# Chunk attention and a two-layer network in one kernel: other block sizes, other early order, transposing DMA from unit 7 on

## The chip, the cores and the metric

The kernel runs on one core of a Trainium2 chip. Its time is the device time of one execution in microseconds; the median of the runs is given. The profile is a separate execution, recorded by the hardware profiler.

## What is computed

Attention inside chunks of 64 positions, for 8 batches, 8 heads, 576 positions and 64 values a head; the heads are then laid side by side to 512 features for 4608 tokens, which go through two matrices with a leaky ReLU between them.

```python
scores = scale * np.matmul(q_c, k_c.transpose(0, 1, 2, 4, 3))   # chunks of 64
scores = scores - np.max(scores, axis=-1, keepdims=True)
attn = np.exp(scores)
attn = attn / (np.sum(attn, axis=-1, keepdims=True) + 1e-09)
out = np.matmul(attn, v_c)
...
x = np.ascontiguousarray(attn_out.transpose(0, 2, 1, 3)).reshape(B * S, H * D)
h = x @ w_in                      # 512 to 2048
g = np.maximum(0.01 * h, h)
return (g @ w_out)                # 2048 to 512
```

## The kernel before

The tokens are cut into 36 units of 128 (two chunks). Each unit goes through stages that the program names with letters:

- **tq, tk**: TensorE transposes q and k into the PSUM tiles qp and kp (one buffer each). **q** copies qp in two halves into QZ, a zero-padded operand, and **k** copies kp into KT, on ScalarE (ACT) or VectorE (DVE). From unit 9 (`UD`) on, q and k come another way: a DMA lays them out and DVE's own transposes (**dq**, **dk**) write QZ and KT.
- **s**: eight matmuls of 64 columns give the scores Sp. **m**, **b**: DVE takes the maximum and subtracts it. **x**: ACT takes the exponential. **z**: DVE sums, adds 1e-9 and inverts (three instructions). **n**: DVE multiplies, which gives the weights en.
- The weights are transposed in one of two ways. Units below `UE`: **e** (four TensorE transposes into tpe) and **c** (a copy out of PSUM into et, ACT or DVE). Units from `UE` on: **d**, one transposing DMA from SP's queue, en to et.
- **v**: eight matmuls of 64 columns of et with V give xp, which shares its one PSUM buffer with tpe. **a**: ACT copies xp into xT, and from then on the unit's tokens count as ready.

The network works on blocks of 128, 256 or 512 tokens (`BLOCKS`). A block is cut into chunks, also called quarters here: `mm1` (4 x 512 columns of the first layer, 16, 8 or 4 matmuls by the size of the block; its activation `act1` on ACT follows) and `mm2` (four matmuls of 512 columns, a quarter of a token tile's second layer). After the fourth quarter `store` copies the tile out of PSUM on ACT and SP's queue stores it. The last tile of all is done by `last`, in pieces. A chunk is 2048 columns whatever the block. There are 288 of them in a list, and a chunk can be taken when all tokens of its block are ready. hT, oP and the idle matmuls share four PSUM buffers.

The order on each engine is the order of the program. It has three stretches. `FRONT` is an order written out by hand: the stages of the first units, `y` and `w` (zeroing), `I` (the identity in fp32, for unit 0), `A`, `G`, `B`, `O` for single chunks of the first blocks (mm1, act1, mm2, store), and `i12`, which is twelve matmuls on the identity whose results are not used. `q1.0.1` means unit 1, half 0, on ACT. Then rounds `it` from 6 to 38 follow: in a round come s, m, b of unit it-1, `fill(2)`, the exponential, the transposes of the next unit's q and k, z and n, another `fill(2)` and `fill(QUARTERS[it] - 4)`, so that `QUARTERS[it]` chunks are taken in a round if the tokens are there. The values (v and a) of a unit come one round after n for units below `UE`, and in the middle of the round after that for the others:

```python
if it - 3 >= UE:
    values(it - 3)
...
if it - 2 < UE:
    values(it - 2)
```

After the rounds `fill(len(chunks))` takes what is left.

The loads are issued on GpSimd's queue in the order of `LOADS`, before all; only unit 0's q and k (q_f, k_f, fp32) come by SP's and ACT's queues.

Of the kernel before, what the change touches and what calls it, by code (L numbers as in the profile page):

```python
# [11 lines left out]
AFT = mybir.ActivationFunctionType  # L12
# [4 lines left out]
def kernel(  # L17
# [9 lines left out]
    nc = tc.nc  # L27

    B, H, S, D = q.shape
    d_model, d_ff = moe_w_in.shape  # L30
# [8 lines left out]
    NVB = 2  # L39
    NIN = 9  # L40
    UD = 9
    UE = 9
    G = 2 * CH

    NU = n_tok // G
    BLOCKS = [128] * 6 + [256] + [128] * 2 + [256] * 5 + [512] * 4

    sbp = ctx.enter_context(tc.tile_pool(name="k_sb", bufs=1))
    psp = ctx.enter_context(tc.tile_pool(name="k_ps", bufs=1, space=bass.MemoryType.PSUM))
# [6 lines left out]
    w_outT = sbp.tile([128, NFC, d_model], FP16, name="w_outT")  # L56
# [87 lines left out]
    oP: dict[tuple[int, int], bass.AP] = {}  # L144
    START = [sum(BLOCKS[:j]) for j in range(len(BLOCKS))]

# [3 lines left out]
    def mm1(j, a):  # L150
        tb, r0 = BLOCKS[j], START[j]
        nf = 512 // tb
        hT = psp.tile([128, nf, tb], FP32, name="hT", tag="mm", bufs=4)
        for i in range(nf):
            fc = nf * a + i
            for t in range(NT):
                nc.tensor.matmul(  # L157
                    out=hT[:, i, :],
                    lhsT=w_inT[:, t, fc * 128:(fc + 1) * 128],
                    rhs=xT[:, t, r0:r0 + tb],  # L160
                    start=(t == 0),
                    stop=(t == NT - 1),
                )
        HT[j, a] = hT

    def act1(j, a):
        tb = BLOCKS[j]
        nf = 512 // tb
        if j not in gT:
            tag, bufs, pad = ("gS", 4, 128) if tb == 128 else ("gT", 2, 512)  # L170
            gT[j] = sbp.tile([128, NFC, tb], FP16, name="gT", tag=tag, bufs=bufs, padded_shape=[128, NFC, pad])
        nc.scalar.activation(  # L172
            out=gT[j][:, nf * a:nf * a + nf, :], in_=HT.pop((j, a)), func=AFT.Prelu, bias=0.0, scale=1.0, alpha=0.01
        )
# [20 lines left out]
        nc.sync.dma_start(out=out[r0:r0 + 128, :], in_=osb)  # L195

    def last(j, ti):
        r0, c = START[j] + ti * 128, d_model // 2
        osb = sbp.tile([128, d_model], FP32, name="osb", tag="osb", bufs=3)
        for h in range(2):  # L200
            o = psp.tile([128, d_model], FP32, name="oP", tag="mm", bufs=4)
            for fc in range(NFC):
                nc.tensor.matmul(  # L203
                    out=o[:, :c],
                    lhsT=gT[j][:, fc, ti * 128:(ti + 1) * 128],
                    rhs=w_outT[:, fc, h * c:(h + 1) * c],
                    start=(fc == 0),
                    stop=(fc == NFC - 1),
                )
            half = slice(h * c, (h + 1) * c)  # L210
            nc.scalar.activation(out=osb[:, half], in_=o[:, :c], func=AFT.Copy, bias=0.0, scale=1.0)  # L211
            nc.sync.dma_start(out=out[r0:r0 + 128, half], in_=osb[:, half])

    def c1(j):
        return [("mm1", j, a, 0) for a in range(NFC * BLOCKS[j] // 512)]

    def c2(j):
        return [("mm2", j, ti, p) for ti in range(BLOCKS[j] // 128) for p in range(NFC // 4)]

    chunks = []  # L220
    for j in range(len(BLOCKS)):
        chunks += c1(j) + c2(j)
    state = {"tokens": 0}

    def fill(n):
        for _ in range(n):
            if not chunks:
                return
            kind, j, a, p = chunks[0]
            if START[j] + BLOCKS[j] > state["tokens"]:  # L230
                return
            chunks.pop(0)
            if kind == "mm1":
                mm1(j, a)
                act1(j, a)
            elif j == len(BLOCKS) - 1 and a == BLOCKS[j] // 128 - 1:
                if p == 0:
                    last(j, a)
            else:
                mm2(j, a, p)  # L240
                if parts[j, a] == NFC // 4:
                    store(j, a)
# [176 lines left out]
    def zero_act(i):  # L419
# [8 lines left out]
            )  # L428

    FRONT = (  # L430
        "y0 y1 y2 y4 w3 I y5 i12 tq0 tk0 q0.1.1 q0.0 tq1 k0.1 q1.0.1 i4 s0 tk1 m0 k1 b0 q1.1.1 i23 s1 x0 "
        "m1 b1 z0 x1 z1 i55 tq2 q2.0.1 n0 i7 tk2 k2 q2.1 i3 e0 n1 c0.1 s2 m2 i3 v0 a0 b2 i12 e1 x2 c1 i9 "
        "v1 z2 A0.0 a1 A1.0 n2 G0.0 e2 A0.1 c2 v2 tq3 a2 A1.1 q3.1 G0.1 q3.0 tk3 A2.0 G1.0 k3.1 G1.1 s3 "
        "A0.2 G2.0 m3 A1.2 b3 x3 A2.1 G0.2 z3 A0.3 G1.2 tq4 G2.1 n3 A1.3 G0.3 e3 G1.3 A2.2 c3 q4.0.1 v3 "
        "tk4 a3 A2.3 k4.1 q4.1 A3.1 y6 G2.3 G2.2 A3.0 G3.1 s4 A3.3 m4 A3.2 b4 G3.3 G3.0 B0.1 G3.2 B3.1 x4 "
        "B0.0 z4 B1.1 n4 B3.0 B1.2 B0.3 tk5 tq5 k5.1 B0.2 q5.1.1 e4 B1.0 O0 c4 q5.0 B1.3 O1 "
    )
    STAGES = {
        "tq": stage_tq, "tk": stage_tk, "q": stage_q, "k": stage_k, "s": stage_s, "m": stage_m, "b": stage_b,
# [6 lines left out]
    def do(name, u):  # L446
        if (name, u) not in done:
            STAGES[name](u)
# [18 lines left out]
    def values(u):  # L467
        if 0 <= u < NU:
            do("v", u)
            do("a", u)  # L470

    QUARTERS = [5] * 8 + [6] * 9 + [7] * 30
    for it in range(6, NU + 3):
        dve = UD <= it < NU
        if it <= NU:
# [5 lines left out]
        fill(2)  # L481
        if it - 3 >= UE:
            values(it - 3)
        if it <= NU:
            do("x", it - 1)
        if it - 2 < UE:
            do("e", it - 2)
# [9 lines left out]
        if it <= NU:  # L497
            do("z", it - 1)
            do("n", it - 1)
            if it - 1 >= UE:  # L500
                do("d", it - 1)
        fill(2)
        if it - 2 < UE:
            values(it - 2)
        fill(QUARTERS[it] - 4)
        for b in range(3, B):
# [33 lines left out]
```

## Time and profile before

| what | value |
|---|---|
| median of 3 runs | 294.11 us (294.11 to 294.14) |
| profiled execution | 294.1 us, its span 292.3 us |
| matmuls, weight loads | 2556 each |
| TensorE busy | 284.4 us |
| VectorE, ScalarE, GpSimd busy | 182.7, 152.5, 119.4 us |
| first matmul, last matmul group | 3.80 us, 285.41 to 288.92 us |

The span runs from the first to the last instruction; 1.8 us of the execution lie around it. A row of the timeline or of the chain begins with its start and its length in microseconds. Matmuls are pipelined, so the length of a single one is longer than its step in a series; the steps are read from the chain, where the ends of a series are set against each other.

### The profile page before, as it was taken

What the parts mean: (1) busy time and instruction counts of PE and PEld (TensorE: products, weight loads), DVE (VectorE), ACT (ScalarE), POOL (GpSimd) and SP (SyncE); (2) the same over time, 40 slices, a digit from 0 to 9 for tenths busy, and PEclk for the clock granted to TensorE, in tenths of its full rate; (3) what the DMA queues carried; (4) which work ended last, traced back from release to release, by engine and by line L of the source; (5) the groups of instructions that cost most, each with busy time, mean ns of one, the idle gap of its engine ahead of it and who ended that gap; (6) DMA issues with size and microseconds to landing.
All of it is one profiled execution on the core that took longest, in us unless ns stands there. A gap on an engine that the chain in (4) does not pass through costs nothing.

```text
span 292.3 us, 6210 instructions
## 1 busy us (share of the span) xinstructions
PE 284.4 (97%) x2556; PEld 181.8 (62%) x2556; DVE 182.7 (63%) x338; ACT 152.5 (52%) x270; POOL 119.4 (41%) x148
## 2 busy tenths in 40 slices
PE   4999999999999999999999999999999999999995
PEld 3989955878677766767676754444454444444444
DVE  5776536879899898888877888787777720000000
ACT  5457713756456545646454547733763387127511
POOL 8857547898509837920394379210000000000000
PEclk9999999999999999999999999999999999999999
DMA  9999999999999999999499999992111320120022
GB/s 131 162 193 194 202 157 184 168 144 146 127 126 61 148 147 135 139 132 99 66 135 138 105 85 148 94 137 90 56 23 31 112 69 0 38 88 21 0 74 72
DMA packets 192332, 32.00 MB, mean 109 GB/s; under 512 B 183472, under 2 KB 187824, under 8 KB 192304
## 3 DMA queue, kind: packets, MB, share of 16 engines
q0 software_dynamic: 170208, 18.10, 114.0%
q1 hardware_dynamic: 21056, 13.24, 19.4%
q8 instruction: 20, 0.33, 0.4%
q10 hardware_dynamic: 1040, 0.26, 0.4%
q14 instruction: 8, 0.07, 0.1%
HBM read 36.70 MB, written 9.44 MB: 158 GB/s over the span
## 4 chain that ended last, share of the span: by engine, by line
PE 97%; POOL 1%; ACT 1%; issue 1%; DVE 0%; POOLq 0%
PE hT L157 43%; PE oP L182 41%; PE Sp L309 3%; PE xp L376 3%; PE idle L396 3%; PE oP L203 1%; PE qp L259 1%; PE tpe L351 1%; PE kp L259 1%; POOL k_in L69 0%; DVE QZ L274 0%; ACT KT L281 0%; ACT QZ L272 0%; POOL q_in L69 0%; ACT osb L211 0%
## 5 line engine op out<-in xcount | busy, mean ns | idle before, releaser
L157 PE MATMUL hT<-xT,w_inT 128*128 128x128 f16 (+2 forms) x1152 | 134.3, 273 | 0.0
L182 PE MATMUL oP<-w_outT,gT 128*128 128x512 f16 x560 | 128.2, 379 | 0.0
L157 PEld LDWEIGHTS <-w_inT 128*128 128x128 f16 x1152 | 90.0, 98 | 32.7
L172 ACT ACTIVATE gT<-hT 128x512 f16<-128x512 f32 x144 | 83.8, 597 | 32.5 <-PE hT L157 32.3
L182 PEld LDWEIGHTS <-gT 128*128 128x128 f16 x560 | 52.3, 98 | 56.3
L193 ACT ACTIVATE osb<-oP 128x512 f32<-128x512 f32 x35 | 20.9, 596 | 64.6 <-PE oP L182 62.7
L87 POOL DMA_DIRECT2D q_d<-in_q_dram x48 | 38.7, 818 | 35.3 <-DVE QZ L291 31.6
L318 DVE TENSOR_REDUCE mx<-Sp 128x8 f32<-128x512 f32 x36 | 24.9, 691 | 31.0 <-PE Sp L309 30.8
L87 POOL DMA_DIRECT2D k_d<-in_k_dram x48 | 38.7, 817 | 2.1 <-DMA q_d<-in_q_dram 1.1
L291 DVE STREAM_TRANSPOSE QZ<-q_d 64x512 f16<-64x512 f16 (+1 forms) x60 | 38.2, 644 | 0.4
L389 ACT ACTIVATE xT<-xp 128x512 f16<-128x512 f32 x36 | 21.4, 594 | 20.6 <-PE xp L376 20.6
L96 POOL DMA_DIRECT2D VB<-in_v_dram x16 | 18.4, 1159 | 20.8 <-PE xp L376 20.5
L334 DVE TENSOR_REDUCE z<-ex 128x8 f32<-128x512 f16 x36 | 23.6, 654 | 4.7 <-ACT ex L328 4.6
L322 DVE TENSOR_TENSOR sh<-Sp,mx 128x512 f32<-128x512 f32 x36 | 24.9, 691 | 1.2
L343 DVE TENSOR_TENSOR en<-ex,zi 128x512 f16<-128x512 f16 x36 | 24.8, 690 | 1.2
L328 ACT ACTIVATE ex<-sh 128x512 f16<-128x512 f32 x36 | 22.6, 628 | 5.3 <-DVE sh L322 5.3
L299 DVE STREAM_TRANSPOSE KT<-k_d 128x512 f16<-128x512 f16 (+1 forms) x30 | 19.4, 654 | 0.8
L376 PEld LDWEIGHTS <-VB 128*128 128x128 f16 x288 | 13.1, 98 | 5.6
L309 PEld LDWEIGHTS <-QZ 128*128 128x128 f16 x288 | 13.2, 99 | 5.4 <-DVE QZ L274 0.2
L309 PE MATMUL Sp<-KT,QZ 128*128 128x64 f16 x288 | 14.5, 195 | 0.1
L376 PE MATMUL xp<-et,VB 128*128 128x64 f16 x288 | 14.3, 193 | 0.0
L396 PE MATMUL idle<-ident 128*128 128x128 f16 x128 | 9.6, 233 | 3.8 <-POOL ident masks.py:199 3.8
(42 smaller groups left out, 104.2 us busy)
## 6 DMA issues: line engine op xcount, KB each, us to landing
out_dram<-osb SPq DMA_DIRECT2D x35, 256.0 KB, 2.3
VB<-in_v_dram POOLq DMA_DIRECT2D x16, 288.0 KB, 6.0
q_d<-in_q_dram POOLq DMA_DIRECT2D x48, 72.0 KB, 6.0
k_d<-in_k_dram POOLq DMA_DIRECT2D x48, 72.0 KB, 5.3
w_inT<-in_moe_w_in_dram POOLq DMA_DIRECT2D x8, 256.0 KB, 9.2
w_outT<-in_moe_w_out_dram POOLq DMA_DIRECT2D x4, 512.0 KB, 9.5
q_in<-in_q_dram POOLq DMA_DIRECT2D x7, 128.0 KB, 9.7
k_in<-in_k_dram POOLq DMA_DIRECT2D x7, 128.0 KB, 9.0
```

The costliest lines, as they stand in the source:

```text
L87: nc.gpsimd.dma_start(out=t[p0:p0 + 32, m, :, :, :].rearrange("p h b d -> p (h b) d"), in_=src[b, h0:h0 + 2, :, dh * 32:dh * 32 + 32].rear ...
L157: nc.tensor.matmul(out=hT[:, i, :], lhsT=w_inT[:, t, fc * 128:(fc + 1) * 128], rhs=xT[:, t, r0:r0 + tb], start=(t == 0), stop=(t == NT - 1),)
L172: nc.scalar.activation(out=gT[j][:, nf * a:nf * a + nf, :], in_=HT.pop((j, a)), func=AFT.Prelu, bias=0.0, scale=1.0, alpha=0.01)
L182: nc.tensor.matmul(out=o, lhsT=gT[j][:, fc, ti * 128:(ti + 1) * 128], rhs=w_outT[:, fc, :], start=(n == 0 and fc == part * 4), stop=(n == ...
L291: nc.vector.transpose(out=qz[s * CH:(s + 1) * CH, :, e0:e0 + n, s, :], in_=qkd[b][0][s * CH:(s + 1) * CH, :, at:at + n * CH].rearrange("p ...
L309: nc.tensor.matmul(out=Sp[:, i, :], lhsT=qz[:, 2 * m + g, e, :, :], rhs=kt[:, 2 * m + g, e, :], start=True, stop=True)
L318: nc.vector.tensor_reduce(out=MX[u], in_=SP[u], axis=AXL.X, op=ALU.max)
L322: nc.vector.tensor_tensor(out=SH[u], in0=SP.pop(u), in1=MX.pop(u).unsqueeze(2).to_broadcast((128, 8, CH)), op=ALU.subtract)
L328: nc.scalar.activation(out=E[u], in_=SH.pop(u), func=AFT.Exp, bias=0.0, scale=SCL)
L334: nc.vector.tensor_reduce(out=z, in_=E[u], axis=AXL.X, op=ALU.add)
L343: nc.vector.tensor_tensor(out=E[u], in0=ex, in1=ZI.pop(u).unsqueeze(2).to_broadcast((128, 8, CH)), op=ALU.mult)
L376: nc.tensor.matmul(out=xp[:, t, e, :], lhsT=VB[b % NVB][:, t, c, :], rhs=et[:, t // 2, e, t % 2, :] if u < UD else et[:, t % 2, e, t // 2, :],
```

## The change

The transposing DMA takes the weights of units 7 and 8 too (`UE` is 7). The list of blocks has six of 128, five of 256 and five of 512 instead of eight, six and four. `QUARTERS` is a list with a number for each round. `FRONT` is another order of the same stages: k's transposes of unit 0 come first, without idles ahead of them, some copies change between ACT and DVE, and the idles are 14, 25, 4, 55, 9, 3, 14 and 5 (129, where there were 128). The last tile is computed in pieces of 256, 128 and 128 columns; the first two are copied by ACT, the third by DVE, and the second is stored from ACT's queue.

```diff
--- before.py
+++ after.py
@@ -39,11 +39,11 @@
     NVB = 2
     NIN = 9
     UD = 9
-    UE = 9
+    UE = 7
     G = 2 * CH
 
     NU = n_tok // G
-    BLOCKS = [128] * 6 + [256] + [128] * 2 + [256] * 5 + [512] * 4
+    BLOCKS = [128, 128, 128, 128, 128, 256, 256, 128, 256, 256, 256, 512, 512, 512, 512, 512]
 
     sbp = ctx.enter_context(tc.tile_pool(name="k_sb", bufs=1))
     psp = ctx.enter_context(tc.tile_pool(name="k_ps", bufs=1, space=bass.MemoryType.PSUM))
@@ -195,21 +195,28 @@
         nc.sync.dma_start(out=out[r0:r0 + 128, :], in_=osb)
 
     def last(j, ti):
-        r0, c = START[j] + ti * 128, d_model // 2
+        r0 = START[j] + ti * 128
         osb = sbp.tile([128, d_model], FP32, name="osb", tag="osb", bufs=3)
-        for h in range(2):
+        for c0, c1, copy, queue in (
+            (0, d_model // 2, nc.scalar, nc.sync),
+            (d_model // 2, 3 * d_model // 4, nc.scalar, nc.scalar),
+            (3 * d_model // 4, d_model, nc.vector, nc.sync),
+        ):
+            part = slice(c0, c1)
             o = psp.tile([128, d_model], FP32, name="oP", tag="mm", bufs=4)
             for fc in range(NFC):
                 nc.tensor.matmul(
-                    out=o[:, :c],
+                    out=o[:, :c1 - c0],
                     lhsT=gT[j][:, fc, ti * 128:(ti + 1) * 128],
-                    rhs=w_outT[:, fc, h * c:(h + 1) * c],
+                    rhs=w_outT[:, fc, part],
                     start=(fc == 0),
                     stop=(fc == NFC - 1),
                 )
-            half = slice(h * c, (h + 1) * c)
-            nc.scalar.activation(out=osb[:, half], in_=o[:, :c], func=AFT.Copy, bias=0.0, scale=1.0)
-            nc.sync.dma_start(out=out[r0:r0 + 128, half], in_=osb[:, half])
+            if copy is nc.vector:
+                copy.tensor_copy(out=osb[:, part], in_=o[:, :c1 - c0])
+            else:
+                copy.activation(out=osb[:, part], in_=o[:, :c1 - c0], func=AFT.Copy, bias=0.0, scale=1.0)
+            queue.dma_start(out=out[r0:r0 + 128, part], in_=osb[:, part])
 
     def c1(j):
         return [("mm1", j, a, 0) for a in range(NFC * BLOCKS[j] // 512)]
@@ -428,12 +435,12 @@
             )
 
     FRONT = (
-        "y0 y1 y2 y4 w3 I y5 i12 tq0 tk0 q0.1.1 q0.0 tq1 k0.1 q1.0.1 i4 s0 tk1 m0 k1 b0 q1.1.1 i23 s1 x0 "
-        "m1 b1 z0 x1 z1 i55 tq2 q2.0.1 n0 i7 tk2 k2 q2.1 i3 e0 n1 c0.1 s2 m2 i3 v0 a0 b2 i12 e1 x2 c1 i9 "
-        "v1 z2 A0.0 a1 A1.0 n2 G0.0 e2 A0.1 c2 v2 tq3 a2 A1.1 q3.1 G0.1 q3.0 tk3 A2.0 G1.0 k3.1 G1.1 s3 "
-        "A0.2 G2.0 m3 A1.2 b3 x3 A2.1 G0.2 z3 A0.3 G1.2 tq4 G2.1 n3 A1.3 G0.3 e3 G1.3 A2.2 c3 q4.0.1 v3 "
-        "tk4 a3 A2.3 k4.1 q4.1 A3.1 y6 G2.3 G2.2 A3.0 G3.1 s4 A3.3 m4 A3.2 b4 G3.3 G3.0 B0.1 G3.2 B3.1 x4 "
-        "B0.0 z4 B1.1 n4 B3.0 B1.2 B0.3 tk5 tq5 k5.1 B0.2 q5.1.1 e4 B1.0 O0 c4 q5.0 B1.3 O1 "
+        "y0 y1 y2 y4 w3 I tk0 y5 tq0 i14 q0.0 q0.1 tq1 k0 q1.0.1 s0 tk1 m0 i25 b0 k1 i4 q1.1.1 s1 x0 m1 "
+        "b1 z0 x1 z1 i55 tq2 q2.0.1 n0 i9 q2.1.1 tk2 e0 k2 s2 n1 c0 i3 m2 v0 b2 i14 a0 x2 e1 c1 i5 z2 v1 "
+        "A0.0 a1 n2 A1.0 G0.0 e2 tq3 c2 A0.1 v2 a2 A1.1 q3.0 G1.1 tk3 A2.0 q3.1 G1.0 k3.1 s3 A1.2 m3 A0.2 "
+        "G2.0 G0.1 b3 x3 A1.3 A2.1 G0.2 z3 A0.3 G2.1 n3 tq4 G1.2 G0.3 e3 tk4 A2.2 c3 G1.3 v3 a3 A2.3 k4 "
+        "q4.0.1 y6 q4.1 A3.1 A3.0 G2.2 G2.3 s4 A3.2 A3.3 B0.0 m4 G3.1 B0.1 b4 G3.3 x4 z4 B3.1 n4 G3.0 "
+        "G3.2 B1.1 B3.0 B0.3 B1.2 tk5 k5 tq5 e4 B0.2 q5.1.1 B1.0 c4 B1.3 O0 q5.0.1 O1 "
     )
     STAGES = {
         "tq": stage_tq, "tk": stage_tk, "q": stage_q, "k": stage_k, "s": stage_s, "m": stage_m, "b": stage_b,
@@ -469,7 +476,7 @@
             do("v", u)
             do("a", u)
 
-    QUARTERS = [5] * 8 + [6] * 9 + [7] * 30
+    QUARTERS = [5, 5, 5, 5, 5, 5, 4, 5, 6, 5, 6, 8, 5, 9, 4, 7, 5, 7, 5, 6, 8, 4, 8, 6, 8, 8, 5, 8, 5, 7, 7, 7, 7, 7, 7, 7, 7, 7, 7, 7, 7, 7, 7, 7, 7, 7, 7, 7, 7]
     for it in range(6, NU + 3):
         dve = UD <= it < NU
         if it <= NU:
```

## The prediction

> **What bounds the kernel now.** I read the page first: the busy shares, then the chain that ended last, then that chain in order of time, and last the timeline of the first 20 us.
>
> ```profile
> span 292.3 us, 6210 instructions
> PE 284.4 (97%) x2556; PEld 181.8 (62%) x2556; DVE 182.7 (63%) x338; ACT 152.5 (52%) x270; POOL 119.4 (41%) x148
> ```
>
> TensorE is busy for all but 8 us. The chain in order of time (start, length, what) shows what a step costs:
>
> ```profile
> 8.20 0.43 PE idle L396 x4
> ...
> 11.18 3.07 PE idle L396 x55
> ...
> 20.91 0.89 PE hT L157 x16
> ...
> 98.62 3.50 PE hT L157 x32
> ...
> 261.24 13.81 PE hT L157 x64
> ...
> 285.41 3.51 PE oP L203 x32
> 288.94 0.38 ACT osb L211
> ```
>
> From these rows, per matmul: 128 columns 55.8 ns (3.07/55, 0.89/16), 256 columns 109.2 ns (3.50/32), 512 columns 215.8 ns (13.81/64). Before 9.5 us 128 columns take 107 ns (0.43/4): the clock is at half although the page's PEclk row says 9. From the first transposes of unit 2's weights (e2, 20.52) to the last matmul the chain is matmuls end to end; no wait of TensorE is listed there. So behind 20.5 us only TensorE work counts, and ahead of it the chain of the first units does. The timeline of that front (start, length, engine, line, operation):
>
> ```profile
> 6.88 0.68 DVE L274 CAST QZ<-qp 64x512 f16<-64x512 f32 x1 [1.75 <-ACT QZ L272]
> 7.62 0.59 PE L259 MATMUL qp<-ident,q_in 128*128 128x128 f16 x4 [0.54 <-DVE QZ L274]
> 8.42 0.64 PE L309 MATMUL Sp<-KT,QZ 128*128 128x64 f16 x8
> 10.13 0.59 ACT L272 ACTIVATE QZ<-qp 64x512 f16<-64x512 f16 x1
> 10.78 0.41 PE L309 MATMUL Sp<-KT,QZ 128*128 128x64 f16 x8
> 14.09 0.39 PE L259 MATMUL qp<-ident,q_in 128*128 128x128 f16 x4
> 14.51 0.59 ACT L272 ACTIVATE QZ<-qp 64x512 f16<-64x512 f16 x1 [1.21 <-PE qp L259]
> 15.25 0.43 DVE L274 COPY QZ<-qp 64x512 f16<-64x512 f16 x1
> 15.28 0.40 PE L351 MATMUL tpe<-ident,en 128*128 128x128 f16 x4
> 15.78 0.39 PE L309 MATMUL Sp<-KT,QZ 128*128 128x64 f16 x8
> 16.36 0.39 PE L376 MATMUL xp<-et,VB 128*128 128x64 f16 x8
> 18.57 1.62 PE L157 MATMUL hT<-xT,w_inT 128*128 128x128 f16 x26
> ```
>
> In order these are: q0's copy, tq1, s0, q1's second half, s1, tq2, q2's halves on ACT and then DVE, e0, s2, v0, and the first real matmul (A0.0) at 18.57. Idle matmuls fill the rest and delay nothing unless they outlast the wait that they cover.
>
> **The front, step by step.** TensorE's queue now begins with tk0, not with twelve idles and tq0. The identity in fp32 is ready at 5.06 (tq0 starts 5.11), but k_f lands 4.6 us after its issue at 0.74 (page part 6; q_f needs 3.9), so tk0 starts at about 5.37, and tq0, 0.90 later (5.11 to 6.01 in the row of four fp32 transposes), at 6.28. Its reader starts 1.15 later (5.11 to 6.26): q0.0 at 7.43. Both halves are now on DVE, 0.68 each, done at 8.75 (ACT and DVE: 7.56 before). tq1 starts 8.82; the 14 idles (14 x 0.107 = 1.5 us, from 7.18) end at 8.68 and are covered. tq1 takes 0.43, so s0 starts at 9.25 against 8.42. If the clock opens at 9.5 as before, tk1 runs 9.63 to 9.85, k1 on ACT from 10.05, q1.1 from 10.66 to 11.25; i25 and i4 (29 x 0.0558 = 1.62) end at 11.47 and set s1: **0.69 later** than 10.78. The DVE chain m1, b1, z0, z1, n0 keeps its order, so e0 comes at 15.97.
>
> TensorE reaches tq2 at 11.47 + 0.23 + 3.07 = 14.77. Behind it ACT now has three copies in a row, q2.0, q2.1, k2, where one half was on DVE: first at 15.19 (14.09 to 14.51 in the rows), 0.61 apart (k1 to q1.1: 9.52, 10.13), the last ends at 17.01. s2 needs k2: 17.06, 1.28 later than 15.78, and TensorE stands still from 16.2. In its queue v0 is behind s2 and i3, although its operand c0, now on DVE, is there at 16.9: v0 at 17.46 (+1.10). Then a0, e1, c1, v1 repeat the old steps (16.36 to 18.57 is 2.21): A0.0 at 19.67. n2 hangs on m2, b2, x2, z2 behind s2: 1.0 later, and A0.0 with A1.0 (1.79) cover it nearly. e2, which waited 0.17 before, comes 0.99 later. **Front: +1.0.** Bounds: +0.8 if ACT's copies go 0.52 apart as three L172 rows do (22.57, 1.57 long), +1.2 if each handover takes 0.05 more. I take the measured 0.61, since those are the same copies.
>
> **TensorE's work behind it.** First layer: blocks of 128 go from eight to six, of 256 from six to five, of 512 from four to five. A block of 128 has 64 matmuls, and so has each other: -128 x 0.0558 - 64 x 0.1092 + 64 x 0.2158 = **-0.32**. Units 7 and 8 lose their four transposes of the weights: -8 x 0.056 = **-0.45**. The last tile: 16 x 0.109 + 32 x 0.056 = 3.54 against 3.49: **+0.05**. Second layer unchanged. Sum -0.72, all of it on the path.
>
> **What hides the moved steps.** DVE loses two copies c (0.42 each). SP gains two DMA transposes, 1.2 us of issue each, 2.4 to 6.1 from issue to landing in the 27 that are there, in a stretch where the DMA row is at 9. Behind them on SP wait only stores, whose three buffers ACT needs back; a store is due about every third chunk pair at most, and none of the 35 rows of L195 shows ACT waiting for a buffer. v7 now comes in round 10 instead of 9, so between n7 and v7 lie round 9 (0.46 + 5 x 0.87 = 4.8) and 2.2 us of round 10: 7.0 against 6.1. Cost nothing; without the cover TensorE would wait the difference. The chunks last too: blocks 0 to 5 (896 tokens) hold 56, the front uses 26, rounds 6 to 10 ask 26 and round 11 two before values 8 opens the next block. The loads (queue order unchanged) meet a later TensorE.
>
> The listed rounds change no work, only the order. The tight ones are the two of four quarters (14 and 21): TensorE passes from one s to the next in 0.46 + 4 x 0.87 = 3.94 us. DVE needs, from s to the end of KT, 3.92 (s at 96.27, KT 99.48 + 0.71) and a handover of 0.05. I take 0.05 for both, bounds 0 and 0.2. Their neighbours (9 and 7, 8 and 8) let DVE, with 5.3 us of work a round, catch up.
>
> **The tail.** Now: ACT copy 0.38 from 288.94, SP's issue 0.33, landing 1.7 after the issue begins. Then: DVE copies 128 columns of fp32. No row shows it; ACT's own 128-column row (L410) is 0.29, and DVE's 512-column cast is 0.68, which scaled by length is 0.17 and with a fixed part nearer 0.28. I take 0.28: -0.10. Landing: 2.0 for 256 KB at the end, 1.7 for 128 KB; for 64 KB I take 1.6. Sum **-0.2**, bounds -0.4 and +0.1. ACT's own issue for the middle piece comes 0.9 us earlier and ends before it.
>
> **Sum** against the profiled execution (294.10, span 292.3 and 1.8 around it; median 294.11): +1.00 - 0.72 + 0.05 - 0.20 = +0.13, so **294.2**. A measurement of this kernel tells about 0.2%, 0.59 us, from no change.
>
> **Rivals.** *The clock opens later (slower).* Place: i25 and i4. TensorE's work begins 1.57 us later (5.37, not 3.80). If the opening moves along, to 11.1, tk1 ends at 10.11, nine idles take 107 ns and twenty 55.8, and s1 comes at 12.22, 0.75 later still: **295.0**. Each us of delay costs 0.48, so it decides from an opening at 10.5. For it: the opening in the trace stands 5.7 us behind the first matmul. Against: in the 3.4 us ahead of it TensorE was busy 2.87 (with a gap at 7.0), and after the change it has no more gaps there; and the three runs and the profile lie within 0.04 us, so the opening did not wander.
> The Trainium skill, "TensorE: Matmul & The Clock Gate", section "What's actually happening", says that the clock opens after one busy window of about 3.4 us and that the windows run free of the kernel's start. By it the opening stays at 9.5 if the windows lie the same, and comes up to one window later, at 12.9, if they lie otherwise; worked as above that is s1 at 13.06 and an estimate of 295.8. The trace agrees with the 107 to 56 ns step and cannot show where the next kernel's windows lie.
> I give the later opening 0.22.
>
> *The front loses little (faster).* If ACT's copies of q2 and k2 did not queue behind one another, or k_f landed with q_f, the 0.72 of saved work would show: with the front at zero 294.10 - 0.72 - 0.2 = **293.2**. It decides when e2 is less than 0.28 later. For it: ACT is idle in half of the span. Against: all three wait for tq2 and tk2, which the 55 idles push behind, and ACT takes them in order. 0.15.
>
> *Short rounds leave DVE behind (slower).* If the small rounds cost 0.3 us each at 12, 14, 16 and 21: +1.2, **295.4**. Against: the 3.94 and 3.92 above, and no round in the trace where TensorE waited for DVE. 0.05.
>
> **How the numbers follow.** The forecast has 0.58; its own range, by the bounds of front, rounds and tail, is 293.8 to 294.8, all within 0.2%. Slower 0.22 + 0.05, faster 0.15. The range reaches to 295.2, past the opening at 11.1, and to 293.6, half of the way to the faster case.
>
> **What would show it.** tk0 first at about 5.4; s1 near 11.5; s2 near 17.1 waiting for ACT's KT; A0.0 near 19.6; e2 near 21.5; from there TensorE without waits, chunk steps as above; the last matmul near 289.2. Wrong if: idles at 107 ns behind 9.6, s2 without a wait, waits of Sp for KT in rounds 14 and 21, or weights' transposes landing behind v7.

## The result

The changed kernel takes 295.09 us (median of 14 runs, 294.29 to 295.95), the kernel before 293.92 in 14 runs (293.63 to 294.14). The ratio is 1.0037 (95% interval 1.0026 to 1.0047): slower by 0.37%. The forecast's range, 293.6 to 295.2, holds it, but its likeliest case, no change at 294.2, did not come. What came is the number of the first rival (a later opening of the clock, that is, of the moment at which the clock granted to TensorE goes from half to full: 295.0), and the experiments show that this rival made only a part of it.

The profiled execution took 294.41. From the page:

```profile
span 292.6 us, 5984 instructions
PE 282.8 (97%) x2437; PEld 173.6 (59%) x2437; DVE 179.8 (61%) x334; ACT 154.2 (53%) x273; POOL 119.3 (41%) x148
```

TensorE has 119 matmuls fewer and is busy 1.6 us less (0.7 of it from e2 on), in a span that is 0.3 longer. The front, from the timeline:

```profile
5.42 1.09 PE L266 MATMUL kp<-ident,k_f 128*128 128x128 f32 x4 [5.42 <-DMA k_f<-in_k_dram]
7.15 1.68 PE L403 MATMUL idle<-ident 128*128 128x128 f16 x14
8.94 0.38 PE L266 MATMUL qp<-ident,q_in 128*128 128x128 f16 x4
11.23 0.40 PE L316 MATMUL Sp<-KT,QZ 128*128 128x64 f16 x8
14.54 0.39 PE L266 MATMUL qp<-ident,q_in 128*128 128x128 f16 x4
14.96 1.20 ACT L279 ACTIVATE QZ<-qp 64x512 f16<-64x512 f16 x2 [1.21 <-PE qp L266]
15.72 0.40 PE L358 MATMUL tpe<-ident,en 128*128 128x128 f16 x4
16.18 0.60 ACT L288 ACTIVATE KT<-kp 128x512 f16<-128x512 f16 x1
16.83 0.39 PE L316 MATMUL Sp<-KT,QZ 128*128 128x64 f16 x8 [0.71 <-ACT KT L288]
19.43 1.95 PE L157 MATMUL hT<-xT,w_inT 128*128 128x128 f16 x32
21.51 0.40 PE L358 MATMUL tpe<-ident,en 128*128 128x128 f16 x4
```

tk0 waits for k_f; the three copies follow one another on ACT from 14.96, and s2 waits for the last (0.71); the first real matmul comes at 19.43 (18.57 before), e2 at 21.51 (20.52). The chain in order of time is no longer TensorE alone. Near 98 us and at the end:

```profile
97.13 1.56 PE oP L182 x8
98.69 6.82 DMA et<-en
105.51 0.04 issue
105.55 0.39 PE xp L383 x8
...
286.02 3.55 PE oP L208 x48
...
289.65 0.29 DVE osb L216
```

A transposing DMA, issued at 98.69, landed 6.82 us later, and v13 waited 0.28 for it. In the tail the last copy is 0.29 (ACT's 0.38 before), and the last store lands 1.56 us after its issue (1.69 before).

### The profile page after: what moved, and what is told of

It reads as the page before. It is cut to its first block, busy times and chain, and to the rows that moved or that the text cites. A ratio compares the mean times of both kernels' runs of the same rounds, so it can differ in the third digit from the quotient of the medians.

```text
span 292.6 us, 5984 instructions
## 1 busy us (share of the span) xinstructions
PE 282.8 (97%) x2437; PEld 173.6 (59%) x2437; DVE 179.8 (61%) x334; ACT 154.2 (53%) x273; POOL 119.3 (41%) x148
## 4 chain that ended last, share of the span: by engine, by line
PE 93%; DMA 4%; DVE 1%; ACT 1%; issue 0%; DVEq 0%; ACTq 0%
PE oP L182 41%; PE hT L157 40%; PE Sp L316 3%; PE xp L383 3%; DMA et<-en 2%; PE idle L403 2%; DMA k_f<-in_k_dram 2%; PE oP L208 1%; PE qp L266 1%; PE kp L266 1%; PE tpe L358 0%; ACT QZ L279 0%; DVE en L350 0%; DVE sh L329 0%; DVE mx L325 0%
## 5 line engine op out<-in xcount | busy, mean ns | idle before, releaser
L157 PEld LDWEIGHTS <-w_inT 128*128 128x128 f16 x1024 | 82.6, 98 | 38.4
L193 ACT ACTIVATE osb<-oP 128x512 f32<-128x512 f32 x35 | 20.9, 596 | 65.7 <-PE oP L182 60.2
L335 ACT ACTIVATE ex<-sh 128x512 f16<-128x512 f32 x36 | 22.6, 628 | 4.0 <-DVE sh L329 3.7
```

The lines of the kernel that those rows point to most:

```text
L157: nc.tensor.matmul(out=hT[:, i, :], lhsT=w_inT[:, t, fc * 128:(fc + 1) * 128], rhs=xT[:, t, r0:r0 + tb], start=(t == 0), stop=(t == NT - 1),)
L335: nc.scalar.activation(out=E[u], in_=SH.pop(u), func=AFT.Exp, bias=0.0, scale=SCL)
```

## The profiles side by side

Behind e2 TensorE stands still only where a step between two matmuls is longer than its kind; those excesses, added up, are the waits. The rest is what is left of the execution time: execution time = start of e2 + waits + rest. The sum holds by this definition; what the thirteen profiles show is that the rest is the same, within 0.03 us, for kernels that have the same work behind e2. The opening of the clock is read from the trace's record of the granted clock. The kernel names are those of the experiments below.

| kernel | first matmul | clock opens | e2 | waits | execution | rest |
|---|---|---|---|---|---|---|
| before | 3.80 | 9.57 | 20.52 | 0 | 294.10 | 273.58 |
| no_idles | 5.11 | 10.44 | 20.90 | 0 | 294.49 | 273.59 |
| tail_alone | 3.79 | 7.83 | 19.96 | 0 | 293.37 | 273.41 |
| after | 5.42 | 8.69 | 21.51 | 0.36 | 294.41 | 272.54 |
| again | 5.48 | 11.54 | 22.59 | 0.59 | 295.73 | 272.55 |
| q2_dve | 5.62 | 11.22 | 22.58 | 0.67 | 295.79 | 272.54 |
| idles_first | 3.79 | 7.76 | 21.47 | 1.34 | 295.36 | 272.55 |
| rounds_moved | 5.39 | 9.41 | 21.53 | 0.02 | 294.09 | 272.54 |
| idles_rounds | 3.79 | 9.04 | 21.59 | 0.03 | 294.14 | 272.52 |
| dma_from_9 | 5.41 | no record (by the steps, between 8.5 and 8.9) | 21.61 | 0.43 | 295.18 | 273.14 |
| front_before | 3.80 | 8.17 | 20.05 | 0.03 | 292.61 | 272.53 |
| front_before_rounds_moved | 3.79 | 8.89 | 20.38 | 0.02 | 292.92 | 272.52 |
| front_before_dma_9 | 3.80 | 9.91 | 20.61 | 0.20 | 293.95 | 273.14 |

Three things can be read here. The rest falls by 1.04 with the whole change, of which 0.17 is the tail (tail_alone against before), 0.60 goes with the transposes of units 7 and 8 (the two kernels with the DMA from unit 9 against 272.54), and 0.27 is left for the blocks. Of the 0.60, 0.46 lie between e2 and the last matmul; the other 0.14 lie behind the last matmul, which is 3.07 to 3.08 us ahead of the span's end with the DMA from unit 7 and 3.21 to 3.22 with the DMA from unit 9 and the same last tile. Why that end is shorter isn't shown. With the front of before e2 runs from 19.96 to 20.90 as the clock opens between 7.83 and 10.44, 0.36 us for each us. With the changed front it stays at 21.5 to 21.6 up to an opening at 9.4 and is at 22.6 with one at 11.2 to 11.5. So the changed front's price depends on the opening: 1.0 at an opening near 9.5, but 1.5 near 7.8 (idles_first against tail_alone), since it makes nothing of an early opening. And the waits differ from one execution to the next, from 0.02 to 1.34.

## Experiments

Every kernel was compared with the kernel before on the same chip, whose median was 293.8 to 293.9 there.

**again**: the changed kernel, unchanged.

> The changed kernel once more, for a second profile. Theory A: its time and the moment at which matmuls of 128 columns go from 107 to 56 ns move together, 0.48 us of time for each us behind about 8.7 (294.4 at 8.69 in the first profile). Theory B: the time moves with waits behind 20 us, and the opening does not matter.

Median 295.03 (294.08 to 295.90), ratio 1.0041 (1.0027 to 1.0056). The front of its chain in order of time:

```profile
5.48 1.09 PE kp L266 x4
6.57 0.85 PE qp L266 x4
7.42 1.49 PE idle L403 x14
...
10.44 2.21 PE idle L403 x29
12.64 0.23 PE Sp L316 x8
...
17.43 0.61 ACT KT L288
18.03 0.04 issue
18.07 0.39 PE Sp L316 x8
```

The 29 idles take 2.21 us; all at 55.8 ns they would take 1.62. s1 is at 12.48 by the timeline, not 11.23. With the opening at 11.54 against 8.69, e2 is 1.08 later. So theory A's mechanism is there, at 0.38 us for each us over this stretch. But 294.41 to 295.73 is 1.32, and another 0.23 are waits of TensorE in v for a transposing DMA, which later experiments call theory C: d8 landed 6.88 us after its issue and v8 waited 0.57.

```profile
68.82 6.88 DMA et<-en
75.70 0.04 issue
75.75 0.41 PE xp L383 x8
```

**no_idles**: the kernel before with `y5 tq0` in place of `y5 i12 tq0`.

> The kernel before without the twelve idle matmuls at its head, so that TensorE's first matmul comes at 5.1 us and not at 3.8; the chain behind it has every start that it had. Theory A (the opening of the clock follows TensorE's first work, and falls anywhere in some 3.4 us): the opening comes up to 1.3 us later, up to 11; median 0.3 to 0.6 over the kernel before, spread up to 1 us where the kernel before has 0.8. Theory B (the opening does not follow the first work): no difference, within 0.1 us.

Median 294.39 (293.91 to 295.41), ratio 1.0022 (1.0011 to 1.0032), so 0.5 us slower for taking away twelve matmuls whose results nobody uses; the runs spread over 1.5 us, not the 1 of the expectation. The chain in order of time:

```profile
5.11 1.13 PE qp L259 x4
...
6.88 0.69 DVE QZ L274
7.57 0.14 issue
7.71 0.58 PE qp L259 x4
...
9.57 1.75 PE idle L396 x23
```

tq0 starts at 5.11 as before; s1 comes at 11.17 (10.78), as the 23 idles are at the half clock up to 10.44. Theory B of this expectation falls.

**idles_first**: the changed kernel with the idles at its head.

```diff
-        "y0 y1 y2 y4 w3 I tk0 y5 tq0 i14 ...
+        "y0 y1 y2 y4 w3 I i12 tk0 y5 tq0 i14 ...
```

> The changed kernel with twelve idle matmuls ahead of tk0, so that TensorE begins at 3.8 us and not at 5.4; nothing else differs, and the idles end at 5.1, before k_f lands. Theory A (the clock opens at a moment that differs from run to run within some 3.4 us, not before TensorE has worked a while; the later TensorE begins, the later it opens): the opening moves back to between 6 and 9.6, the median falls to about 294.35 and the spread of the runs from 1.7 us to at most 0.5. Theory B (the cost and the spread are in the order of the front and in the rounds, clock aside): nothing changes, 294.3 to 296, median 295.1.

Median 294.52 (294.29 to 295.36), ratio 1.0030 (1.0019 to 1.0042). The interval overlaps that of again, so the medians alone don't decide. The profile does say where it fell short: the clock opened at 7.76 and e2 came at 21.47, and yet this was the slowest of its seven runs, because v7 waited 0.31 and v8 1.01 (d7 and d8 landed 7.4 and 7.3 us after their issue):

```profile
60.03 0.23 PE xp L383 x8
61.24 14.09 DMA et<-en x2
75.38 0.41 PE xp L383 x8
```

So half of theory A's expectation failed: the spread did not end with the early opening. That led to theory C, the transposing DMAs.

**rounds_moved**: one chunk from round 11 to 10, one from 13 to 14.

```diff
-    QUARTERS = [5, 5, 5, 5, 5, 5, 4, 5, 6, 5, 6, 8, 5, 9, 4, 7, ...
+    QUARTERS = [5, 5, 5, 5, 5, 5, 4, 5, 6, 5, 7, 7, 5, 8, 5, 7, ...
```

> The changed kernel with one chunk moved from round 11 to round 10 and one from round 13 to round 14, which puts 0.87 us more between the transposing DMAs of units 8 and 13 and their readers v8 and v13. Theory C (besides the front, TensorE waits in v for DMAs that land 5 to 7 us after their issue): the waits of 0.05 to 1.3 us near 74 and of 0.3 near 105 vanish; median 0.4 to 0.7 under the changed kernel, and a spread of what the opening alone makes, 1.2 us or so. Theory A alone: no difference.

Median 294.09 (293.79 to 295.24), ratio 1.0015 (1.0004 to 1.0026): 0.9 under again, more than expected (the means, 294.38 and 295.09, lie 0.7 apart). The same DMA rows land as late, and nothing waits for them:

```profile
DMA to landing us min/median/max: 2.4/4.2/7.1
```

The waits behind e2 are 0.02. The runs still spread over 1.45 us; the opening alone made 1.08 between after and again, but no profile of so slow a run of this kernel was taken.

**idles_rounds**: both edits.

> The changed kernel with the twelve idles ahead of tk0 and the moved chunks together. In the profiles so far, execution time = start of e2 + waits of TensorE behind it + 272.54. With no waits behind e2 and the clock open by 9.6, e2 stands at 21.1 to 21.6: 293.7 to 294.2 in the profile, median 294.0, spread at most 0.6. If the early idles do nothing for the opening: 294.1 and a spread of 1.4 as with the moved chunks alone.

Median 293.99 (293.81 to 294.50, 12 runs), ratio 1.0005 (0.9997 to 1.0014): as expected in the median (the spread is 0.7), and no longer to be told from the kernel before. The highest run is 294.50 against 295.24 without the early idles.

**dma_from_9**: the changed kernel with `UE = 9`.

> The changed kernel with units 7 and 8 back on TensorE's transposes (UE is 9), the rest as changed. By TensorE's work 0.45 slower. Theory C: the wait of v8 vanishes (0.05 to 1.3), so that the median moves by -0.4 to +0.3; the spread shrinks. Theory A alone: 0.45 over the changed kernel, 295.5.

Median 295.13 (294.32 to 295.73), ratio 1.0043 (1.0027 to 1.0060), within theory C's range; it does not tell the theories apart by its time, for its interval holds again's. Its profile has no wait at v7 or v8, but 0.32 at e3, which the changed kernel's profile lacks, and 0.09 at a later v; its rest is 0.60 higher. The DMAs cost about what they saved.

**q2_dve**: `q2.1` in place of `q2.1.1`, unit 2's second half on DVE.

> The changed kernel with unit 2's second half of q copied by DVE as before, not by ACT. By the chain of the front, k2 then ends 0.6 earlier and s2 no longer waits 0.9 us for it, but m2 and c0 then stand behind the copy and n1 on DVE: 0.2 to 0.6 under the changed kernel at the same opening of the clock. Theory A: the spread stays near 1.7 us, with a median of 294.5 to 294.9. Theory B (front order is all): the median falls by 0.6 and the spread shrinks.

Median 294.96 (294.57 to 295.79), ratio 1.0038 (1.0025 to 1.0051): no gain that could be measured. From its timeline:

```profile
16.92 0.43 DVE L281 COPY QZ<-qp 64x512 f16<-64x512 f16 x1
17.38 0.69 DVE L350 TENSOR_TENSOR en<-ex,zi 128x512 f16<-128x512 f16 x1
17.50 0.39 PE L316 MATMUL Sp<-KT,QZ 128*128 128x64 f16 x8 [0.15 <-ACT KT L288]
...
18.11 0.42 DVE L367 COPY et<-tpe 128x512 f16<-128x512 f16 x1
18.45 0.68 DVE L325 TENSOR_REDUCE mx<-Sp 128x8 f32<-128x512 f32 x1
18.59 0.39 PE L383 MATMUL xp<-et,VB 128*128 128x64 f16 x8 [0.53 <-DMA q_in<-in_q_dram]
```

s2 waits 0.15 and not 0.7. But the copy pushes n1 back on DVE, c0 (et, done at 18.53) stands behind n1, and v0 starts just behind c0 at 18.59; the view puts its 0.53 of waiting down to a load, but c0 ended last. m2 is behind c0 too. e2 is at 22.58, the same as in again at nearly the same opening. The wait at s2 was only the first of two.

**front_before**: the changed kernel with the FRONT of before.

> The changed kernel with the FRONT of before; blocks, DMA from unit 7, rounds and last tile as changed. Theory A: the front costs all, and the rest saves 0.72 in TensorE's work and 0.4 in the tail less 0.3 of waits in the rounds, so 0.8 under before: about 293.1, spread at most 0.5, the opening at 9.6 or earlier. Theory B with the cost in the rounds: 294.5 or more.

Median 293.09 (292.60 to 294.11, 12 runs), ratio 0.9974 (0.9965 to 0.9984): the expectation's median to the tenth, but not its terms. It counted on 0.4 from the tail, on waits of 0.3 in the rounds and on a spread of at most 0.5; the tail gives 0.17, the profile's waits are 0.03, and the runs spread over 1.5. All of the change but the front is, together, a gain.

**front_before_rounds_moved**: that front and the moved chunks.

> The FRONT of before and the moved chunks together, the rest as changed. Theory C: the front of before runs 1.4 us earlier by then, and its profile had no wait in v, but d8 and d13 stand close to their readers there too: 0 to 0.4 under the 293.1 of the front alone, so 292.7 to 293.1, with the smallest spread of all. Theory A alone: 293.1.

Median 292.90 (292.50 to 293.09), ratio 0.9967 (0.9955 to 0.9979), the lowest of all and under both kernels by their intervals. Against front_before alone the intervals overlap.

**front_before_dma_9**: the FRONT of before and `UE = 9`, the rest as changed.

> The FRONT of before and the transposing DMA from unit 9 as before; blocks, rounds and last tile as changed. Against the front of before alone (293.1): TensorE's transposes of units 7 and 8 cost 0.45 and the waits of v8 are gone; 293.3 to 293.5 if those waits are rare with this front, 293.1 if they cost as much as the transposes save.

Median 293.87 (293.23 to 294.32), ratio 0.9998 (0.9989 to 1.0008), 0.8 over front_before where 0.2 to 0.4 were expected. The opening in its profile, 9.91, is the latest with this front, and the rest is 0.60 higher, not 0.45. With this front the DMA from unit 7 is a clear gain.

**tail_alone**: the kernel before with the new `last`.

> The kernel before with the last tile in three pieces and nothing else. From the two profiles: 0.05 more of TensorE's work, 0.35 less from the last matmul to the end: 0.30 under the kernel before, ratio 0.9990. A tail that the store's landing alone sets: 0 to -0.1.

Ratio 1.0002 (0.9993 to 1.0010): too small to see beside the run-to-run spread. The rest of its profile is 0.17 lower, half of the 0.30.

## Why the prediction was right or wrong

**TensorE's work: right.** -0.32, -0.45 and +0.05 were predicted for blocks, transposes and last tile; between e2 and the last matmul the profiles give -0.27, -0.46 and +0.04. From e2 to the last matmul's end, waits left out, it is 267.69 against 268.38: -0.69 for -0.72.

**The front: right in its steps, at the opening that it took.** tk0 at 5.42 (5.37), s2 at 16.83 (17.06), A0.0 at 19.43 (19.67), e2 at 21.51 (21.51), with a wait for ACT's KT where it was put. That e2 agrees to the hundredth is chance: s1 and s2 came 0.24 and 0.23 early, as the clock opened at 8.69 and not at 9.5, and one DVE instruction of unit 2 (ze, L343) took 0.34 where it takes 0.17 in most profiles. Compared at one opening (before at 9.57, rounds_moved at 9.41), e2 is 1.01 later: +1.0 was forecast. At earlier openings it costs up to 1.5, which the prediction, with one opening in hand, did not see. What one would conclude from its steps, that s2's wait is the thing to mend, was wrong: q2_dve took most of it away and the next wait held e2.

**The tail: right.** -0.20 was predicted behind the last matmul, besides the +0.05 of its matmuls; tail_alone's profile gives -0.21 and +0.04, -0.17 together. The first pair of profiles shows -0.34 behind the last matmul (tail_alone's expectation took this, as 0.35, for the tail's gain); 0.13 to 0.14 of it go with the DMA of units 7 and 8, as above.

**"The opening did not wander": wrong.** This step took four executions of one kernel at 294.1 for proof. The same kernel runs from 293.52 to 294.59 beside the experiments, and the openings lie at 7.76 to 9.91 where TensorE begins at 3.8, at 8.69 to 11.54 where it begins at 5.1 or later. The rival had the mechanism, but the opening does not simply move along by 1.57: it fell anywhere in 2.2 us with the early start (seven profiles) and in 2.9 us that begin 0.9 later with the late one (five). The price of 0.48 for each us fits only past 9.4 (1.06 later for 2.13, from rounds_moved to again); ahead of that, e2 hardly moves. Here the Trainium skill ("TensorE: Matmul & The Clock Gate", "What's actually happening") was the better guide: it says that the windows run free of the kernel's start. The trace agrees: from opening to falling back are 283.306 us in eleven traces and 286.720 in one, 83 and 84 windows of its 3.413 us.

**"Cost nothing" for the moved DMAs: wrong.** The step worked out the cover of unit 7 (7.0 us against landings of up to 6.1; the profiles give 6.9 to 7.4 from issue to v7) and not that of unit 8. From d8's issue to where v8 would start without a wait are 6.3 to 6.5 us in the five profiles with the changed rounds, and d8 landed after 5.3 to 7.3: v8 waited in the three of them in which it took about 6.5 or more. The bound of 6.1 was the slowest of 27 that did not include this stretch; d7 took up to 7.4. The rival of the short rounds looked at DVE and KT: those waits are 0.02 to 0.03, as forecast. Yet a short round did cost 0.28 in the first profile: with four chunks in round 14, v13 stands 6.6 us behind d13's issue (7.6 before), and d13 took 6.8. The 35 rows of L195 in that paragraph are the issues of the stores; the copies that would wait for a buffer are L193's, and the profile of before has no wait of theirs for a store.

**The sum.** In the first profile: +0.99 front, +0.36 waits, -1.04 rest, +0.31 in all, for the +0.13 forecast. The median is 0.7 above that profile, since the opening came early in it and v8 hardly waited (0.05). How the two share the median isn't measured run by run: without the waits it falls by 0.9 (the mean by 0.7), and with the early idles besides by 0.1 more (the mean by 0.3), mostly in the spread. That the range holds the median is in part luck: it was stretched to 295.2 for an opening at 11.1, while the time came from openings between 8.69 and 11.54 together with waits that the prediction had put at nothing.

## What to carry to other kernels

Work that fills time ahead of the first data on TensorE is not for nothing where the clock opens late: judge it by the moment at which the step of a matmul halves, over several profiles, and not by one. When a transfer replaces work on the bound engine, work out the time from issue to reader for every unit that moves, and set it against the slowest landing in the same stretch, with some to spare; here one chunk moved for each of the two late transfers was enough. An edit of many parts is best undone part by part: here the other parts together were a gain, and one, the early order, cost more than all of it.

## What the runs showed of the hardware that was not expected

The clock opened 3.3 to 6.1 us after TensorE's first matmul, at another point in each of the twelve profiles that recorded it; between two executions of the changed kernel this alone moved e2 by 1.08 us. The transposing DMA from SP's queue took 2.4 to 2.5 us from issue to landing in 107 of the 114 cases, over all profiles, in which no load of GpSimd's queue was under way, and up to 7.4 (d7 in idles_first) among the loads of q, k and v. That those loads are what holds it up is inferred, not tested.
